# Another order of the ELU, the dot products and the weight rounding inside a dense step of a fused attention, MLP and expert kernel

## The chip, the cores and the metric

The kernel runs on one core of one Trainium2 chip. The time is device time in microseconds (us), from launch to end, of one execution; the figure for a kernel is the median of several executions. Five engines work side by side: TensorE (PE, with its weight loads shown as PEld), VectorE (DVE), ScalarE (ACT), GpSimd (POOL) and SyncE (SP), which issues most transfers. Each engine runs its own instructions in the order in which the program wrote them, and waits on semaphores for the others.

## The reference, cut to what matters

```python
def _attn_ref(q, k, v):      # 2 batches, 8 heads, 768 positions, 64 dims:
    ...                      # local window plus block summaries, softmax
def _moe_ref(x, w_in, w_out):            # 1536 tokens, 512 -> 2048 -> 512
    h = x @ w_in
    g = np.where(h > 0.0, h, alpha * (np.exp(np.minimum(h, 0.0)) - 1.0))
    return (g @ w_out).astype(np.float32)

def _moe2_ref(x, expert_emb, tau, w1, w2):   # 8 experts, 512 -> 1024 -> 512
    xn = x / (np.linalg.norm(x, axis=-1, keepdims=True) + 1e-06)
    en = expert_emb / (np.linalg.norm(expert_emb, axis=-1, keepdims=True) + 1e-06)
    logits = xn @ en.T / tau
    expert_idx = np.argmax(logits, axis=1)
    ...
    for e in range(E):
        h = np.maximum(x[mask] @ w1[e], 0.0)
        out[mask] = gate_w[mask, None] * (h @ w2[e])
```

The change lies in `_moe_ref` (the dense MLP with its ELU) and in the products with the expert embeddings that choose an expert for each token.

## The kernel before

Attention comes first, then 64 **dense steps**, then 64 **expert steps**. A dense step `g` takes one of four chunks of 384 tokens (batch 0 and 1, two chunks each) and one of 16 slices of 128 hidden units. Steps 32 to 47 are the first chunk of batch 1, steps 48 to 63 the second. Expert steps begin at `GD` = 64.

To keep 32-bit precision, every operand is split in a rounded part and the rest: `split_hi` (L186, ACT) writes the rounded weights, `split_lo` (L190, DVE or POOL) the difference. A product is then three matmuls: high by high, high by low, low by high. In a step

- `up` (L557 to L559) is the first product, 12 matmuls into a PSUM bank `hp`;
- the ELU of the step before (`prev`) follows: `act_a` (L564, ACT: the negative part of `hp` into a tile `e`), `act_b` (L569, ACT: the exponential), `act_max` (L573, DVE: the maximum with `hp`), `act_hi` (L577, ACT: the rounded activations `gt`), `act_lo` (L581, POOL: the rest of `gt`);
- `split_u` rounds the weights of the first product two steps ahead; call its parts u_hi (ACT) and u_lo (DVE);
- `split_d` rounds the weights of the second product, d_hi (ACT) and d_lo (POOL in most steps from 33 on, DVE in steps 55 to 57);
- `down` (L596 to L598) is the second product of step `g - 2`, 9 matmuls.

So the activations of step `s` are made while step `s + 1` is issued, and multiplied in step `s + 2`.

Beside this, `extra` holds work that is hung on a step: from step 33 on the dot products `y_dot` of finished outputs with the expert embeddings. An output tile is loaded from memory two steps earlier (`y_load`, SP, tile `yl`). At its first dot product ACT copies it to PSUM (`yp`, L636); each of eight dot products (L640, DVE) reads `yp` and the embeddings `en_b`; after the first, ACT squares it (`ysq`, L630). Steps 33 to 40 hold four dot products each, steps 41 to 46 three (the last of them one), steps 52 to 54 one, 55 to 59 four. Routing, scatter, gather and the transposes of the first expert slot are in `extra` too (steps 49 to 64).

The order inside a step is that of the code, for each engine: `up`, `act_a`, `split_u`, `split_d` of the step before, `act_b`, `act_c` (which is `act_max`, `act_hi`, `act_lo`), loads, `extra`, `down`. Every instruction waits in its engine's queue for those written ahead of it.

Of the kernel before, what the change touches and what calls it, by code (L numbers as in the profile page):

```python
# [81 lines left out]
def fused_kernel(ctx, tc, q, k, v, w_in, w_out, emb, tau, w1, w2, consts, toks, minit, out):  # L82
    nc = tc.nc
# [48 lines left out]
    VP, RAW, BITS = {}, {}, {}  # L132
# [25 lines left out]
    def conv_bits(f, *ops):  # L158

        for n, o in ops:  # L160
            if f not in VP:
                VP[f] = v_p.tile([P, PW], F32, tag="v", name="vt")
            raw = RAW[f, n]
            hi, lo = raw[:, :, 1], raw[:, :, 0]
            t = VP[f][:, n * 512:(n + 1) * 512].bitcast(I32)
            if o == 0:
                BITS[f, n] = bank("cv").bitcast(I32)
            m = BITS[f, n]
            if o == 0:
                nc.vector.tensor_scalar(out=m, in0=hi, scalar1=3, scalar2=None, op0=ALU.logical_shift_left)  # L170
            if o == 1:
                nc.vector.scalar_tensor_tensor(
                    out=m, in0=hi, scalar=-0x80000000, in1=m, op0=ALU.bitwise_and, op1=ALU.bitwise_or
                )
            if o == 2:
                nc.vector.scalar_tensor_tensor(  # L176
                    out=t, in0=lo, scalar=29, in1=m, op0=ALU.logical_shift_right, op1=ALU.bitwise_or
                )
# [4 lines left out]
    def split_hi(src, down=False):  # L183
        pool, tag = (late["p"], "wd") if down and late else (w_p, "w")
        wt = pool.tile([P, 2, 512], F32R, tag=tag, name="wt", bufs=5)
        nc.scalar.activation(out=wt[:, 0, :], in_=src, func=AF.Copy)  # L186
        return wt

    def split_lo(src, wt, eng):
        eng.tensor_tensor(out=wt[:, 1, :], in0=src, in1=wt[:, 0, :].bitcast(F32), op=ALU.subtract)  # L190

    def split(src, eng, down=False):
        wt = split_hi(src, down)
        split_lo(src, wt, eng)
        return wt
# [342 lines left out]
    class Dense:  # L538
# [5 lines left out]
            self.eng = nc.gpsimd if (b, c) == (0, 0) else nc.vector  # L544

        def split_u(self):
            self.u = split(VP[self.f][:, 0:512], self.eng)

        def split_d(self, pool):
            self.d = split(VP[self.f][:, 512:1024], nc.gpsimd if pool else self.eng, True)  # L550

        def up(self):
            wt, xt = self.u, XT[self.b, self.c]
# [306 lines left out]
    class Expert:  # L860
# [16 lines left out]
            self.v = t  # L877

        def split_u(self):
            self.u = split(self.v[:, 0:512], nc.vector)  # L880

        def split_d(self, pool=False):
            self.d = split(self.v[:, 512:1024], nc.gpsimd if pool else nc.vector, True)

        def up(self):
            wt, x = self.u, self.s.x
# [103 lines left out]
    steps = [Dense(b, c, f) for b in range(B) for c in range(NCH) for f in range(KF)]  # L990
# [86 lines left out]
    with tc.manual_schedule():  # L1077
# [10 lines left out]
        GD = len(steps)  # L1088
        steps += [None] * (B * NSTAT * KE)
        GN = len(steps)  # L1090
        extra = {}
# [70 lines left out]
        for i in range(1, B * NSTAT):  # L1162
            g = GD + i * KE
            slot_steps(i, max(g - LEAD - 2, g1 + 3 if i >= NSTAT else 0), max(g - 7, g1 + 8 if i == NSTAT else 0), g - 3)
        pool_d = [32 < g <= 48 or 48 < g < g0 + 6 or g0 + 9 <= g < GD or GD < g < g1 + 5 and (g - GD) % KE not in (2,) for g in range(GN + 2)]

        def load_piece(g):
            s, f = divmod(g - GD, KE)
            steps[g] = (Expert if slots[s].tiles == NT2 else Half)(slots[s], f)
            steps[g].load()  # L1170

        n_split = G0 + 1
        for g in range(G0, GN + 2):
            prev = steps[g - 1] if 0 <= g - 1 < GN else None
            if g < GN:
                steps[g].up()
            if prev:
                prev.act_a()
                if g > GD and not isinstance(prev, Half):
                    prev.act_c()  # L1180
            if g - 3 >= GD and steps[g - 3].f == KE - 1:
                steps[g - 3].s.put()
            while n_split <= min(g + (1 if g < KF else 2), GN - 1):
                steps[n_split].split_u()
                n_split += 1
            one = isinstance(prev, Half)
            if g == GN:
                prev.split_d()
            if one:
                prev.act_c()  # L1190
            if prev and g < GN:
                prev.split_d(pool_d[g] and not one)
            if g < KF - 2:
                conv_bits(g + 2, *ALL[:3])
            if prev:
                prev.act_b()
                if g <= GD:
                    prev.act_c()
            if GD <= g + LEAD < GN:
                load_piece(g + LEAD)  # L1200
            for fn in extra.get((g, False), []):
                fn()
            if g >= 2:
                steps[g - 2].down()
            for fn in extra.get((g, True), []):
                fn()
# [94 lines left out]
```

## Time and profile before

| what | value |
|---|---|
| median of 3 runs | 562.68 us (561.32 to 563.0) |
| profiled execution, its own time | 561.42 us |
| its span, first to last instruction | 559.6 us |
| PE busy (matmuls) | 517.4 us, 92% of the span |
| DVE busy | 425.7 us, 76% |
| ACT busy | 354.0 us, 63% |
| POOL busy | 270.7 us, 48% |
| mean granted TensorE clock | 0.984 |

Step 33 begins at 233.86 us of the span with its first L557 matmul, step 37 at 250.59, step 44 at 286.76, step 59 at 349.78; step 64, the first expert step, begins at 372.49. Matmuls overlap, so their busy time says little about pauses; the start of one step to the start of the next says how long a step held PE. In an answer on a stretch, a row's "idle" with an arrow names what ended the wait just before that instruction.

### The profile page before, as it was taken

The page shows a single profiled execution, that of the slowest core. Times are in us where ns is not written, and L with a number is a line of the kernel's source. Part 1 is how long each engine was busy: PE and PEld are TensorE (multiplying, and loading weights), DVE is VectorE, ACT ScalarE, POOL GpSimd, SP SyncE. Part 2 cuts the span into 40 slices and gives each one's busy share as a digit, 9 for nine tenths or more (in the row PEclk, how much of TensorE's full clock was granted, in tenths as well). Part 3 has the DMA queues.
Part 4 walks back from the last instruction along what each step waited for, and adds up shares of the span by engine and source line. Part 5 has one row for each costly group of instructions (what it writes and reads, how often), then busy time and mean ns, then how long its engine had stood idle before and what let it go on. Part 6 is the DMA issues. An engine that isn't in the chain of part 4 may idle for free.

```text
span 559.6 us, 10282 instructions
## 1 busy us (share of the span) xinstructions
PE 517.4 (92%) x3270; PEld 455.2 (81%) x3270; DVE 425.7 (76%) x1053; ACT 354.0 (63%) x870; POOL 270.7 (48%) x274
## 2 busy tenths in 40 slices
PE   4986898999899999998999999999999999999991
PEld 4765786879788898896888998889779989999980
DVE  4999999988997665488776488866899777656671
ACT  3888685666767675565476655665565586566570
POOL 1477686876385332344457546765376532121010
PEclk9999998999999999999999999999999999999997
DMA  8999865669302014020100223718946399965000
GB/s 216 205 262 218 301 216 201 177 168 218 108 1 53 20 35 169 20 77 19 37 2 2 75 57 95 249 54 281 340 163 208 111 339 316 335 215 181 20 29 14
DMA packets 98939, 81.28 MB, mean 145 GB/s; under 512 B 38159, under 2 KB 83599, under 8 KB 98368
## 3 DMA queue, kind: packets, MB, share of 16 engines
q1 hardware_dynamic: 96256, 73.72, 44.7%
q0 software_dynamic: 2624, 6.84, 3.4%
q8 instruction: 28, 0.46, 0.4%
q14 instruction: 31, 0.25, 0.2%
HBM read 73.03 MB, written 6.94 MB: 143 GB/s over the span
## 4 chain that ended last, share of the span: by engine, by line
PE 31%; issue 8%; DVE 7%; ACT 5%; POOL 3%; POOLq 0%; ACTq 0%; DVEq 0%
PE shp L891 3%; PE o L914 3%; PE shp L892 3%; PE shp L890 3%; PE o L915 3%; PE o L913 3%; DVE ydj L640 3%; POOL wt L190 2%; DVE e L573 2%; PE y L598 1%; ACT wt L186 1%; DVE wt L190 1%; PE y L596 1%; PE y L597 1%; ACT gt L577 1%
## 5 line engine op out<-in xcount | busy, mean ns | idle before, releaser
L581 POOL TENSOR_TENSOR gt<-e,gt 128x384 fp32r<-128x384 f32 x63 | 64.0, 1016 | 87.7 <-ACT gt L577 50.1
L190 POOL TENSOR_TENSOR wt<-vt,wt 128x512 fp32r<-128x512 f32 x60 | 79.5, 1333 | 39.4 <-ACT wt L186 35.1
L190 DVE TENSOR_TENSOR wt<-mv,wt 128x512 fp32r<-128x512 f32 x113 | 80.6, 750 | 15.3 <-ACT wt L186 8.2
L557 PE MATMUL hp<-xT,wt 128*128 128x384 f32 x256 | 86.8, 339 | 3.8 <-DVE vt L176 2.7
L186 ACT ACTIVATE wt<-vt 128x512 fp32r<-128x512 f32 x128 | 75.5, 626 | 21.9 <-PE y L598 11.9
L559 PE MATMUL hp<-xT,wt 128*128 128x384 f32 x256 | 86.8, 339 | 0.2
L558 PE MATMUL hp<-xT,wt 128*128 128x384 f32 x256 | 86.3, 337 | 0.6 <-DVE xT L456 0.6
L598 PE MATMUL y<-wt,gt 128*128 128x512 f32 x192 | 77.9, 406 | 3.0 <-POOL gt L581 2.0
L596 PE MATMUL y<-wt,gt 128*128 128x512 f32 x192 | 78.7, 410 | 1.8 <-ACT gt L577 1.8
L190 DVE TENSOR_TENSOR wt<-vt,wt 128x512 fp32r<-128x512 f32 x68 | 57.7, 861 | 29.4 <-ACT wt L186 29.2
L577 ACT ACTIVATE gt<-e 128x384 fp32r<-128x384 f32 x64 | 33.5, 524 | 71.2 <-DVE e L573 67.3
L597 PE MATMUL y<-wt,gt 128*128 128x512 f32 x192 | 76.3, 398 | 0.0
L186 ACT ACTIVATE wt<-mv 128x512 fp32r<-128x512 f32 x128 | 73.8, 629 | 0.0
L640 DVE SCALAR_TENSOR_TENSOR ydj<-yp,en_b 128x512 bf16<-128x512 f32 x72 | 46.4, 686 | 12.6 <-ACT yp L636 5.9
L890 PE MATMUL shp<-sx,wt 128*128 128x256 f32 x192 | 54.4, 283 | 1.0 <-DVE ydj L640 0.7
L891 PE MATMUL shp<-sx,wt 128*128 128x256 f32 x192 | 54.2, 282 | 0.3 <-DVE sx L845 0.3
L557 PEld LDWEIGHTS hp<-xT,wt 128*128 128x128 f32 x256 | 48.4, 189 | 7.4 <-issue 2.4
L892 PE MATMUL shp<-sx,wt 128*128 128x256 f32 x192 | 54.0, 281 | 0.0
L558 PEld LDWEIGHTS hp<-xT,wt 128*128 128x128 f32 x256 | 48.5, 189 | 3.5 <-DVE xT L456 0.9
L598 PEld LDWEIGHTS y<-wt,gt 128*128 128x128 f32 x192 | 36.5, 190 | 16.1 <-POOL gt L581 6.9
L559 PEld LDWEIGHTS hp<-xT,wt 128*128 128x128 f32 x256 | 48.3, 189 | 1.0 <-POOL wt L190 1.0
L400 ACT ACTIVATE pt<-pt,mn 128x120 f32<-128x120 f32 x96 | 36.6, 384 | 13.9 <-DVE mn L395 13.2
(175 smaller groups left out, 1194.6 us busy)
## 6 DMA issues: line engine op xcount, KB each, us to landing
mv<-in_moe_w_dram SPq DMA_DIRECT2D x128, 256.0 KB
rw<-in_moe_w_in_dram SPq DMA_DIRECT2D x16, 512.0 KB
rv<-in_moe_w_out_dram SPq DMA_DIRECT2D x13, 512.0 KB
vw<-in_v_dram SPq DMA_DIRECT2D x16, 240.0 KB
kn<-in_k_dram SPq DMA_DIRECT2D x16, 192.0 KB
qn<-in_q_dram SPq DMA_DIRECT2D x16, 192.0 KB
vst<-in_v_dram SPq DMA_DIRECT2D x4, 768.0 KB
y_d<-ysb SPq DMA_DIRECT2D x12, 256.0 KB
```

The costliest lines, as they stand in the source:

```text
L186: nc.scalar.activation(out=wt[:, 0, :], in_=src, func=AF.Copy)
L190: eng.tensor_tensor(out=wt[:, 1, :], in0=src, in1=wt[:, 0, :].bitcast(F32), op=ALU.subtract)
L557: nc.tensor.matmul(hp, wh, xt[:, 0, kk, :], start=(kk == 0), stop=False)
L558: nc.tensor.matmul(hp, wh, xt[:, 1, kk, :], start=False, stop=False)
L559: nc.tensor.matmul(hp, wl, xt[:, 0, kk, :], start=False, stop=(kk == KD - 1))
L581: eng.tensor_tensor(out=gt[:, 1, :], in0=self.e, in1=gt[:, 0, :].bitcast(F32), op=ALU.subtract)
L596: nc.tensor.matmul(yp, gh, woh, start=(f == 0), stop=False)
L597: nc.tensor.matmul(yp, gh, wol, start=False, stop=False)
L598: nc.tensor.matmul(yp, gl, woh, start=False, stop=(f == KF - 1))
L890: nc.tensor.matmul(hp, wh, x[:, 0, kk, :], start=(kk == 0), stop=False)
L891: nc.tensor.matmul(hp, wh, x[:, 1, kk, :], start=False, stop=False)
L892: nc.tensor.matmul(hp, wl, x[:, 0, kk, :], start=False, stop=(kk == KD - 1))
```

## The change

In steps 33 to 64 the order within a step is written anew. `act_b` comes right behind `act_a`; then the first half of the step's `extra`; then `act_max`; then u_hi, d_hi, `act_hi`, `act_lo`, d_lo, the loads, u_lo, and the second half of `extra`. The `split_d` of a step is now issued in the step itself and not in the next one: step 33 issues those of 32 and 33, and step 65 none. `split_u` and `split_d` are taken apart into a `_hi` and a `_lo` part for this, in the dense and the expert class alike. No instruction is added or left out.

```diff
+        ELU0 = 33
         for g in range(G0, GN + 2):
             prev = steps[g - 1] if 0 <= g - 1 < GN else None
+            dense = ELU0 <= g <= GD
+            one = isinstance(prev, Half)
+            todo = extra.get((g, False), [])
...
+            if dense:
+
+                prev.act_b()
+                for fn in todo[:len(todo) // 2]:
+                    fn()
+                prev.act_max()
+                todo = todo[len(todo) // 2:]
...
+            new = []
             while n_split <= min(g + (1 if g < KF else 2), GN - 1):
-                steps[n_split].split_u()
+                if dense:
+                    steps[n_split].split_u_hi()
+                    new.append(steps[n_split])
+                else:
+                    steps[n_split].split_u()
                 n_split += 1
...
-            if prev and g < GN:
+            if dense:
+                ds = steps[g if g > ELU0 else g - 1:g + 1]
+                for x in ds:
+                    x.split_d_hi()
+                prev.act_hi()
+                prev.act_lo()
+                for x in ds:
+                    x.split_d_lo(pool_d[g])
+            elif prev and g < GN and g != GD + 1:
                 prev.split_d(pool_d[g] and not one)
...
-            if prev:
+            if g < ELU0:
                 prev.act_b()
-                if g <= GD:
-                    prev.act_c()
+                prev.act_c()
             if GD <= g + LEAD < GN:
                 load_piece(g + LEAD)
-            for fn in extra.get((g, False), []):
+            for x in new:
+                x.split_u_lo()
+            for fn in todo:
                 fn()
```

On VectorE, step 37 (and the head of step 38) stands like this before. `wt` is the result of a weight rounding, here u_lo; `e` with `hp` is the maximum of step 36, `ydj` a dot product with the copy `yp`.

```order
L190 TENSOR_TENSOR wt_3052<-vt_1089,wt_3052 128x512
L573 SCALAR_TENSOR_TENSOR e_3050<-e_3050,hp_2994 128x384
L640 SCALAR_TENSOR_TENSOR ydj_3065,lr_2788<-yp_3063,en_b_2828 128x512
L640 SCALAR_TENSOR_TENSOR ydj_3069,lr_2788<-yp_3063,en_b_2828 128x512
L640 SCALAR_TENSOR_TENSOR ydj_3071,lr_2788<-yp_3063,en_b_2828 128x512
L640 SCALAR_TENSOR_TENSOR ydj_3073,lr_2788<-yp_3063,en_b_2828 128x512
L190 TENSOR_TENSOR wt_3103<-vt_1123,wt_3103 128x512
```

The same step of the changed kernel on VectorE, with the head of step 38:

```order
L654 SCALAR_TENSOR_TENSOR ydj_3058,lr_2788<-yp_3056,en_b_2828 128x512
L654 SCALAR_TENSOR_TENSOR ydj_3062,lr_2788<-yp_3056,en_b_2828 128x512
L587 SCALAR_TENSOR_TENSOR e_3053<-e_3053,hp_2997 128x384
L190 TENSOR_TENSOR wt_3065<-vt_1089,wt_3065 128x512
L654 SCALAR_TENSOR_TENSOR ydj_3074,lr_2788<-yp_3056,en_b_2828 128x512
L654 SCALAR_TENSOR_TENSOR ydj_3076,lr_2788<-yp_3056,en_b_2828 128x512
L654 SCALAR_TENSOR_TENSOR ydj_3107,lr_2788<-yp_3056,en_b_2828 128x512
```

Two dot products moved ahead of the maximum, and u_lo from ahead of the maximum to right behind it.

On ScalarE, step 37 before (`wt` here are u_hi and d_hi, in that order):

```order
L564 ACTIVATE e_3050<-hp_2994 128x384
L186 ACTIVATE wt_3052<-vt_1089 128x512
L186 ACTIVATE wt_3055<-vt_926 128x512
L569 ACTIVATE e_3050<-e_3050 128x384
L577 ACTIVATE gt_3060<-e_3050 128x384
L636 ACTIVATE yp_3063<-yl_2983 128x512
L630 ACTIVATE ysq_3067,ss_2787<-yp_3063 128x512
```

And in the changed kernel:

```order
L578 ACTIVATE e_3053<-hp_2997 128x384
L583 ACTIVATE e_3053<-e_3053 128x384
L650 ACTIVATE yp_3056<-yl_2986 128x512
L644 ACTIVATE ysq_3060,ss_2787<-yp_3056 128x512
L186 ACTIVATE wt_3065<-vt_1089 128x512
L186 ACTIVATE wt_3067<-vt_972 128x512
L591 ACTIVATE gt_3069<-e_3053 128x384
```

The exponential moved past both roundings, and the copy and the square past `gt`, which is now the step's last instruction on this engine; d_hi reads the next slice (`vt_972` for `vt_926`).

On GpSimd, steps 37 and 38 and the head of 39 before:

```order
L190 TENSOR_TENSOR wt_3055<-vt_926,wt_3055 128x512
L581 TENSOR_TENSOR gt_3060<-e_3050,gt_3060 128x384
L190 TENSOR_TENSOR wt_3106<-vt_972,wt_3106 128x512
L581 TENSOR_TENSOR gt_3111<-e_3101,gt_3111 128x384
L190 TENSOR_TENSOR wt_3149<-vt_1048,wt_3149 128x512
```

And in the changed kernel, from the last instruction of step 36 on:

```order
L190 TENSOR_TENSOR wt_3020<-vt_926,wt_3020 128x512
L595 TENSOR_TENSOR gt_3069<-e_3053,gt_3069 128x384
L190 TENSOR_TENSOR wt_3067<-vt_972,wt_3067 128x512
L595 TENSOR_TENSOR gt_3116<-e_3104,gt_3116 128x384
L190 TENSOR_TENSOR wt_3114<-vt_1048,wt_3114 128x512
```

Within a step d_lo stood ahead of the rest of `gt`; it now stands behind it, and belongs to the next slice.

## Rows read from the trace of the kernel before

**Rows 1.** Windows, four stretches of steps: us, busy us (and count) of each engine.

```profile
core 0: us, PE busy (x) PEld busy (x) DVE busy (x) ACT busy (x) POOL busy (x), PEclk, DMA share, GB/s
233.86:250.59 16.73, 16.73 (x86) 15.14 (x84) 11.95 (x31) 11.50 (x26) 7.52 (x7) 1.00 0.18 64
250.59:286.76 36.17, 33.37 (x148) 27.05 (x147) 30.27 (x73) 20.39 (x45) 18.16 (x16) 0.95 0.07 22
286.76:349.78 63.02, 63.02 (x328) 56.84 (x327) 45.05 (x129) 40.97 (x89) 37.19 (x37) 1.00 0.17 51
349.78:372.49 22.71, 22.45 (x115) 19.36 (x113) 16.33 (x34) 14.30 (x32) 17.27 (x16) 1.00 0.58 187
390.00:430.00 40.00, 37.76 (x249) 32.95 (x248) 38.06 (x91) 21.07 (x48) 21.92 (x20) 1.00 0.78 254
```

**Rows 2.** Timeline of TensorE: start us, us, line, operation, wait before it.

```profile
233.86 0.33 PE L557 MATMUL hp<-xT,wt 128*128 128x384 f32 x1
...
238.04 0.33 PE L557 MATMUL hp<-xT,wt 128*128 128x384 f32 x1
...
263.69 0.50 PE L596 MATMUL y<-wt,gt 128*128 128x512 f32 x1 [1.25 <-ACT gt L577]
...
364.93 0.60 PE L841 MATMUL stp<-cst,xg 128*128 128x128 f32 x4
...
372.49 0.39 PE L890 MATMUL shp<-sx,wt 128*128 128x256 f32 x1 [0.22 <-ACT sx L844]
373.21 0.39 PE L891 MATMUL shp<-sx,wt 128*128 128x256 f32 x1 [0.34 <-DVE sx L845]
```

**Rows 3.** Timeline of VectorE, ScalarE and GpSimd, steps 37 to 39.

```profile
251.76 0.54 DVE L573 SCALAR_TENSOR_TENSOR e<-e,hp 128x384 f32<-128x384 f32 x1
...
254.35 1.30 POOL L190 TENSOR_TENSOR wt<-vt,wt 128x512 fp32r<-128x512 f32 x1 [0.35 <-ACT wt L186]
...
254.67 1.53 DVE L190 TENSOR_TENSOR wt<-vt,wt 128x512 fp32r<-128x512 f32 x1
256.12 0.54 DVE L573 SCALAR_TENSOR_TENSOR e<-e,hp 128x384 f32<-128x384 f32 x1
...
257.80 0.69 DVE L640 SCALAR_TENSOR_TENSOR ydj<-yp,en_b 128x512 bf16<-128x512 f32 x1 [1.14 <-ACT yp L636]
...
258.54 0.60 ACT L630 ACTIVATE ysq<-yp 128x512 f32<-128x512 f32 x1 [0.77 <-DVE ydj L640]
...
259.26 0.69 DVE L640 SCALAR_TENSOR_TENSOR ydj<-yp,en_b 128x512 bf16<-128x512 f32 x1 [0.75 <-ACT ysq L630]
...
259.87 0.69 DVE L640 SCALAR_TENSOR_TENSOR ydj<-yp,en_b 128x512 bf16<-128x512 f32 x1
...
261.10 1.46 DVE L190 TENSOR_TENSOR wt<-vt,wt 128x512 fp32r<-128x512 f32 x1
262.48 0.54 DVE L573 SCALAR_TENSOR_TENSOR e<-e,hp 128x384 f32<-128x384 f32 x1
```

**Rows 4.** Groups by line in steps 33 to 43: busy us, mean ns, idle before.

```profile
L190 DVE TENSOR_TENSOR wt<-vt,wt 128x512 fp32r<-128x512 f32 x11 | 12.6, 1148 | 0.8 <-ACT wt L186 0.8
...
L581 POOL TENSOR_TENSOR gt<-e,gt 128x384 fp32r<-128x384 f32 x10 | 10.2, 1015 | 12.6 <-ACT gt L577 10.6 <-issue 1.7 <-POOL wt L190 0.3
...
L569 ACT ACTIVATE e<-e 128x384 f32<-128x384 f32 x11 | 5.7, 520 | 0.0
L564 ACT ACTIVATE e<-hp 128x384 f32<-128x384 f32 x10 | 4.8, 480 | 0.0
```

**Rows 5.** Tile `wt`, 232 to 256 us: ns min/median/max of the roundings on VectorE.

```profile
L190 DVE TENSOR_TENSOR wt<-vt,wt x5: 691/1467/1535, 233.6 to 254.7; 128x512 fp32r<-128x512 f32 x5
```

**Rows 6.** Timeline: an output tile's load on SyncE and its copy, steps 35 to 37.

```profile
243.47 0.32 SPq L616 DMA_DIRECT2D yl<-y_d  x1
...
246.40 0.59 ACT L636 ACTIVATE yp<-yl 128x512 f32<-128x512 f32 x1
```

**Rows 7.** Timeline of VectorE in step 61: one u_lo.

```profile
359.58 3.27 DVE L190 TENSOR_TENSOR wt<-vt,wt 128x512 fp32r<-128x512 f32 x1 [0.94 <-ACT wt L186]
```

More of the change, by code (lines that the diff above doesn't have):

```diff
@@ L546, in split_u, with split_u_hi, split_u_lo, split_d_hi @@
         def split_u(self):
[L547 to L550 removed]
+            self.split_u_hi()
+            self.split_u_lo()
+        def split_u_hi(self):
+            self.u = split_hi(VP[self.f][:, 0:512])
+        def split_u_lo(self):
+            split_lo(VP[self.f][:, 0:512], self.u, self.eng)
+        def split_d(self, pool):
+            self.split_d_hi()
+            self.split_d_lo(pool)
+        def split_d_hi(self):
+            self.d = split_hi(VP[self.f][:, 512:1024], True)
+        def split_d_lo(self, pool):
+            split_lo(VP[self.f][:, 512:1024], self.d, nc.gpsimd if pool else self.eng)
         def up(self):
@@ L879, in split_u, with split_u_hi, split_u_lo, split_d_hi @@
         def split_u(self):
-            self.u = split(self.v[:, 0:512], nc.vector)
-        def split_d(self, pool=False):
-            self.d = split(self.v[:, 512:1024], nc.gpsimd if pool else nc.vector, True)
+            self.split_u_hi()
+            self.split_u_lo()
+        def split_u_hi(self):
+            self.u = split_hi(self.v[:, 0:512])
+        def split_u_lo(self):
+            split_lo(self.v[:, 0:512], self.u, nc.vector)
+        def split_d(self, pool=False):
+            self.split_d_hi()
+            self.split_d_lo(pool)
+        def split_d_hi(self):
+            self.d = split_hi(self.v[:, 512:1024], True)
+        def split_d_lo(self, pool):
+            split_lo(self.v[:, 512:1024], self.d, nc.gpsimd if pool else nc.vector)
         def up(self):
@@ L1178, in fused_kernel @@
                 prev.act_a()
-                if g > GD and not isinstance(prev, Half):
+                if g > GD and not one:
                     prev.act_c()
+            if dense:
[4 more added lines that the diff above has]
+                todo = todo[len(todo) // 2:]
             if g - 3 >= GD and steps[g - 3].f == KE - 1:
                 steps[g - 3].s.put()
+            new = []
             while n_split <= min(g + (1 if g < KF else 2), GN - 1):
-                steps[n_split].split_u()
+                if dense:
[3 more added lines that the diff above has]
+                    steps[n_split].split_u()
                 n_split += 1
-            one = isinstance(prev, Half)
             if g == GN:
```

## Prediction

> **What bounds the kernel now.** I first looked at the windows of the steps that the change touches [rows 1] and at the starts of single steps on TensorE [rows 2]. Step 33 begins at 233.86 us and step 34 at 238.04: a step with nothing in its way takes 4.18 us. The windows give the rest by subtraction. Steps 33 to 36 take 16.73 us, which is 4 x 4.18: no pause. Steps 37 to 43 take 36.17, where 7 x 4.18 is 29.26: PE stands for **6.91 us**. Steps 44 to 58 take 63.02 against 62.70: nothing (the routing's few matmuls lie there). Steps 59 to 63 take 22.71 against 20.90, 1.81 more; two sets of four transposes lie in it, each busy for 0.60 us [rows 2], so 0.6 to 1.8 is pause, and I take **1.1**. At the first matmuls of step 64 PE waits 0.22 + 0.34 us [rows 2], **0.56**. In sum PE stands for about **8.6 us** between 233 and 374 us, and this is all that the change can win where it acts. Elsewhere in the stretch PE issues without a gap, so work taken from another engine there is worth nothing.
>
> Who makes PE wait? At 263.69 it waits 1.25 us for `gt` from ACT [rows 2], and `gt` is late because the maximum on DVE is. The timeline of DVE shows the beat: the maximum comes at 251.76, 256.12 and 262.48 [rows 3], so two steps with four dot products each take DVE 10.72 us, where PE needs 8.36. DVE falls behind by 1.18 us a step from step 33 on; once the lead of the first steps is used up (by step 37), PE waits. This lasts until the dot products become three a step (step 41). In the window of these stalls the granted TensorE clock averages 0.95, in the other stretches it is 1.00 [rows 1]: part of the 6.91 us is matmuls at the lower of the clock's two levels, 1.2 GHz, after the pause at 262 to 263 us, and goes with the pause.
>
> **What fills the 10.72 us** [rows 3]. Eight dot products, one every 0.61 us (259.26 to 259.87): 4.88. Two maxima at 0.54: 1.08. Two u_lo, 1.53 and 1.46: 2.99. One wait of 1.14 for the copy `yp` and one of 0.75 for the square, both on ACT. That is 10.84, and ends that overlap take 0.1 off.
>
> **The change, part by part.**
>
> *u_lo behind the maximum.* Now u_lo begins while POOL works on d_lo (254.35 to 255.65 against 254.67 to 256.20, [rows 3]). In this part of the trace it took 0.69 us at best and 1.47 in the median [rows 5], and over steps 33 to 43 1.148 in the mean, 11 times [rows 4]. In the new order POOL's block of a step starts with the rest of `gt`, which needs `gt` (0.53 us on ACT), which needs the maximum; u_lo starts directly at the maximum's end. So it has a lead of 0.5 us and needs 0.69, and POOL's block (1.02 + 1.30, [rows 3, 4]) is over 2.9 us behind the maximum, well ahead of the next. Bounds: 0.69 (alone) and 1.53 (as now). I take 0.69, since nearly all of it lies where POOL is idle: 2.99 becomes 1.38.
>
> The Trainium skill (SBUF — State Buffer, section "SBUF: two separate sides") says that VectorE and GpSimd share one pair of SBUF ports as an exclusive lock, taken for a whole instruction by a VectorE operation with two SBUF inputs. The trace agrees in kind, 0.69 against 1.47 us in rows 5; by the rule and by the rows the sum is the same as long as u_lo comes first, and the rule's other case is the third rival below.
>
> *The exponential first, the copy ahead of `gt`.* Now `yp` stands on ACT behind `gt`, and DVE idles 1.14 us from the maximum to the first dot product. In the new order DVE has u_lo and two dot products to do after the maximum (0.69 + 1.22 = 1.91 us), while ACT does `gt` (0.53), the negative part (0.48), the exponential (0.52, [rows 4]) and the copy (0.59, [rows 6]): 2.12. The wait falls from 1.14 to about 0.2; its bounds are 0 and 1.14.
>
> *The square* keeps its place between the first and second dot product: 0.75 as now.
>
> *Half the dot products ahead of the maximum.* They cost DVE nothing more, but the maximum, `gt`, its rest and `down` stand behind them, and behind `yp` and the square. What hides this: activations made in step s + 1 are needed in step s + 2, and PE has 2 x 4.18 = 8.36 us of other matmuls between. The chain in a step with a copy is 0.48 + 0.52 + 0.59 + 0.69 + 0.60 + 0.69 + 0.54 + 0.53 + 1.02 = 5.66 us, with about 0.1 for each of nine handovers (ysq begins 0.05 after the dot product's end, the next dot product 0.12 after ysq's, [rows 3]) 6.6. So 1.8 us to spare; without it each step would stop PE.
>
> *d_hi and d_lo one step earlier, d_lo behind the rest of `gt`.* Their number stays, and d_lo's 1.30 us [rows 3]; the weights are ready a step sooner, and `gt`'s rest no longer stands behind 1.30 us of d_lo. Step 33 rounds two slices (about 0.6 us more on ACT, an estimate from the copy of as many elements, [rows 6]), and step 65 none; ACT is busy 11.5 of 16.7 us there [rows 1] and hides it. Zero either way.
>
> *Loads.* `y_load` keeps its place, two steps ahead; SP is passed by nothing else that PE waits for. Scatter and gather on POOL (steps 55 to 59) now stand ahead of the rest of `gt`; POOL is busy 37 of 63 us there [rows 1], and the spare time covers them.
>
> **Sum.** Two steps on DVE: 4.88 + 1.08 + 1.38 + 0.2 + 0.75 = 8.29 us against PE's 8.36. DVE stops falling behind, though by a hair. Of the 6.91 us I count 6.6; 0.3 is left for step 40, which has the small normalising operations on DVE besides its four dot products. Of 1.1 + 0.56 in steps 59 to 64 I count 1.2: there too u_lo meets POOL (one took 3.27 us, [rows 7]) and the maximum and the slot's copies stand behind the roundings. Together **7.8 us**. The profiled execution took 561.42 us, 1.26 less than the median of the three runs (562.68) and inside their spread: 553.6 by its own time, 554.9 by the median. I say **554.3 us**.
>
> **Rivals.**
> 1. *The forecast.* DVE keeps PE's beat. 554.3 us; chance 0.66.
> 2. *u_lo still meets POOL as now.* If u_lo keeps about 1.5 us (POOL's block of the step before not over, or u_hi late), two steps take 8.29 + 1.6 = 9.9 us, 1.5 too long; four such pairs (steps 33 to 40) make 6.2, less the 1.8 to spare 4.4 us of PE waits, 4.1 more than forecast: 558.4 us. For it: the beat fits by only 0.07 us. Against: POOL's block ends 1.3 us before the next maximum. Chance 0.18.
> 3. *Slower: u_lo falls behind POOL's joined block.* Where u_lo starts more than about 0.5 us behind the maximum, the rest of `gt` and d_lo are on POOL one behind the other, and u_lo ends only after both, 2.3 us later; the 3.27 us of rows 7 is such a case. In steps 33 to 40 a pair would take 8.29 + 4.6 = 12.9 us, 4.5 too long, 18 for the four pairs less 1.8: 16 us of waits where 6.6 were to be won, about 570 us. It decides if u_hi, which stands ahead of `gt` on ACT, is not done when the maximum ends. Against it: u_hi, about as long as the copy (0.59 us, [rows 6]), follows the exponential or the square at once. Chance 0.04. It is the lock of the Trainium skill's page on SBUF taken by the other side first.
> 4. *A late tile in front of the maximum (slower).* Each of nine `yl` loads now stands ahead of a maximum. To end 0.3% above before, they would have to come some 1.1 us beyond the spare 1.8 each: 564.4 us. Against it: one issued at 243.47 was used at 246.40 [rows 6], 2.9 us at most, and two steps are 8.4. Chance 0.03.
> 5. *Won and given back.* From 390 to 430 us DVE is busy 38.06 of 40 us [rows 1]; if expert steps that start 8 us sooner only wait longer there, 561 to 562 us. Against it: that work hangs on steps and moves along with them. Chance 0.07.
>
> The remaining 0.02 I spread.
>
> **How the numbers follow.** About 0.3% (1.7 us) is what a measurement of this kernel can tell from no change. Faster are 1 and 2 and a little of the rest: 0.86; no change is 5: 0.07; slower 3 and 4: 0.07. The range begins where all 8.6 us go and some of the small waits behind step 64 with them, 552.2, and ends at the second rival with the copy's wait at its upper bound, 558.8; it leaves out 3, 4 and 5.
>
> **What would show each step.** In the profile after: steps 37 to 43 in some 29.5 us and the clock at 1.00 throughout; u_lo at 0.7 us in the mean instead of 1.148; maxima two steps apart by 8.4 us; the first dot product's wait for `yp` near 0.2; `gt` on ACT waiting little for the maximum. If PE still waits for `gt` in steps 38 to 42, step 2 holds; if it waits for weights (`wt` from DVE), step 3. The prediction is wrong if the expert steps take longer than before from start to end, or if dot products wait for a load.

## The result, and the profile after

The changed kernel takes **553.0 us** in the median of 4 runs (552.34 to 555.01), the kernel before 562.62 us (561.32 to 563.0, 4 runs beside it): a ratio of 0.9839, 95% interval 0.9807 to 0.9871, **1.6% faster**. Run a second time with other kernels it gave 554.16 us, ratio 0.9848 (0.9814 to 0.9883). Its profiled execution took 553.61 us with a span of 551.8; before, 561.42 and 559.6. So the span is 7.8 us shorter.

The windows of the changed kernel, the same five stretches as [rows 1] (steps 33 to 36, 37 to 43, 44 to 58, 59 to 63, and 40 us of expert steps):

```profile
core 0: us, PE busy (x) PEld busy (x) DVE busy (x) ACT busy (x) POOL busy (x), PEclk, DMA share, GB/s
234.12:250.85 16.73, 16.73 (x86) 15.14 (x85) 14.82 (x39) 13.82 (x31) 9.06 (x8) 1.00 0.18 64
250.85:280.06 29.21, 29.21 (x149) 26.41 (x147) 25.65 (x70) 20.91 (x46) 17.94 (x17) 1.00 0.09 28
280.06:343.08 63.02, 63.02 (x329) 56.85 (x327) 49.58 (x126) 42.33 (x87) 37.99 (x38) 1.00 0.20 59
343.08:364.85 21.77, 21.77 (x114) 19.62 (x113) 13.57 (x30) 14.14 (x30) 13.56 (x13) 1.00 0.51 172
382.40:422.40 40.00, 37.71 (x248) 32.91 (x247) 38.06 (x92) 21.19 (x48) 21.87 (x20) 1.00 0.77 254
```

Steps 37 to 43 take 29.21 us, which is 7 x 4.18 within 0.05, where they took 36.17: PE no longer stands, and the granted clock is 1.00 where it was 0.95. That is 6.96 us. Some 1.7 of them are the clock, an estimate from this window of the kernel before (columns as above): right behind PE's waits in step 39 TensorE ran 3.42 us at a granted 0.50, the lower of the clock's two levels (1.2 GHz), in place of 1.00.

```profile
264.84:268.26 3.42, 3.42 (x9) 2.74 (x10) 2.58 (x6) 1.37 (x4) 1.42 (x2) 0.50 0.24 77
```

Steps 59 to 63 take 21.77 for 22.71, 0.94 less, and PE is busy all of it, so what is above 20.90 is the transposes. The other stretches are as long as before. Step 64 waits once instead of twice [rows 2] (timeline of TensorE):

```profile
364.85 0.28 PE L918 MATMUL shp<-sx,wt 128*128 128x256 f32 x1
...
365.47 0.39 PE L919 MATMUL shp<-sx,wt 128*128 128x256 f32 x1 [0.34 <-DVE sx L859]
```

From the first matmul of step 33 to that of step 65 it is 134.85 us, where it was 142.87: **8.0 us** gained, some 6.3 of pauses and 1.7 of clock. Step 33 itself began 0.26 us later (234.12 for 233.86). From step 65 to the end of the span nothing changed (182.83 us and 182.87).

The beat of VectorE, and GpSimd beside it, against [rows 3] (timeline, two steps with four dot products each):

```profile
253.34 0.55 DVE L587 SCALAR_TENSOR_TENSOR e<-e,hp 128x384 f32<-128x384 f32 x1
...
253.81 0.68 DVE L190 TENSOR_TENSOR wt<-vt,wt 128x512 fp32r<-128x512 f32 x1
...
254.41 0.68 DVE L654 SCALAR_TENSOR_TENSOR ydj<-yp,en_b 128x512 bf16<-128x512 f32 x1
...
254.53 1.02 POOL L595 TENSOR_TENSOR gt<-e,gt 128x384 fp32r<-128x384 f32 x1 [2.36 <-ACT gt L591]
...
255.51 1.29 POOL L190 TENSOR_TENSOR wt<-vt,wt 128x512 fp32r<-128x512 f32 x1
...
256.86 0.55 DVE L587 SCALAR_TENSOR_TENSOR e<-e,hp 128x384 f32<-128x384 f32 x1
...
257.32 0.68 DVE L190 TENSOR_TENSOR wt<-vt,wt 128x512 fp32r<-128x512 f32 x1
...
259.42 0.69 DVE L654 SCALAR_TENSOR_TENSOR ydj<-yp,en_b 128x512 bf16<-128x512 f32 x1 [0.20 <-ACT yp L650]
...
260.87 0.69 DVE L654 SCALAR_TENSOR_TENSOR ydj<-yp,en_b 128x512 bf16<-128x512 f32 x1 [0.75 <-ACT ysq L644]
...
261.49 0.55 DVE L587 SCALAR_TENSOR_TENSOR e<-e,hp 128x384 f32<-128x384 f32 x1
```

From maximum to maximum two steps later it is 8.15 us (253.34 to 261.49; 8.21 one step earlier), where it was 10.72 and PE needs 8.36. Each u_lo takes 0.68, directly behind the maximum; the first ends at 254.49, GpSimd starts at 254.53 and is done at 256.80, ahead of the next u_lo at 257.32. The wait for `yp` is 0.20, that for the square 0.75 as before.

The groups by line in steps 33 to 43 (against [rows 4]):

```profile
L595 POOL TENSOR_TENSOR gt<-e,gt 128x384 fp32r<-128x384 f32 x11 | 11.5, 1047 | 19.3 <-ACT gt L591 11.8 <-issue 6.1 <-PE hp L573 0.9
L190 DVE TENSOR_TENSOR wt<-vt,wt 128x512 fp32r<-128x512 f32 x11 | 8.6, 784 | 0.0
...
L591 ACT ACTIVATE gt<-e 128x384 fp32r<-128x384 f32 x11 | 5.7, 522 | 6.0 <-DVE e L587 6.0
```

The mean u_lo is 784 ns, 1148 before. Two are long: in step 34 (1.21 us), where GpSimd still works on the second d_lo of step 33, and in step 42 (1.26 us), whose maximum comes only 2.3 us behind that of step 41, so that GpSimd still works on step 41's d_lo.

### The profile page after: what moved, and what is told of

It is laid out like the page before. It is cut to its first block, busy times and chain, and to the rows that moved or that the text cites. A ratio compares the mean times of both kernels' runs of the same rounds, so it can differ in the third digit from the quotient of the medians.

```text
span 551.8 us, 10263 instructions
## 1 busy us (share of the span) xinstructions
PE 511.1 (93%) x3270; PEld 453.2 (82%) x3270; DVE 425.7 (77%) x1053; ACT 357.1 (65%) x870; POOL 268.5 (49%) x274
## 4 chain that ended last, share of the span: by engine, by line
PE 66%; DVE 14%; issue 6%; DMA 4%; ACT 3%; SPq 3%; POOL 3%; POOLq 0%; ACTq 0%; DVEq 0%
PE y L610 6%; PE y L612 6%; PE y L611 6%; PE hp L573 6%; PE hp L571 6%; PE hp L572 6%; PE shp L919 4%; PE shp L920 4%; PE shp L918 4%; PE o L942 3%; PE o L943 3%; PE o L941 3%; DVE cv L172 3%; DVE cv L170 3%; PE sc L383 2%
## 5 line engine op out<-in xcount | busy, mean ns | idle before, releaser
L595 POOL TENSOR_TENSOR gt<-e,gt 128x384 fp32r<-128x384 f32 x63 | 65.3, 1036 | 108.0 <-ACT gt L591 62.1
L190 DVE TENSOR_TENSOR wt<-mv,wt 128x512 fp32r<-128x512 f32 x114 | 81.9, 755 | 14.1 <-ACT wt L186 12.2
L610 PE MATMUL y<-wt,gt 128*128 128x512 f32 x192 | 77.6, 404 | 1.7 <-ACT gt L591 1.7
L612 PE MATMUL y<-wt,gt 128*128 128x512 f32 x192 | 76.1, 397 | 1.6 <-DVE gt L595 0.8
L611 PE MATMUL y<-wt,gt 128*128 128x512 f32 x192 | 75.6, 394 | 0.0
L190 DVE TENSOR_TENSOR wt<-vt,wt 128x512 fp32r<-128x512 f32 x67 | 51.7, 785 | 14.3 <-ACT wt L186 14.1
```

The costliest lines, as they stand in the source:

```text
L595: eng.tensor_tensor(out=gt[:, 1, :], in0=self.e, in1=gt[:, 0, :].bitcast(F32), op=ALU.subtract)
L610: nc.tensor.matmul(yp, gh, woh, start=(f == 0), stop=False)
L611: nc.tensor.matmul(yp, gh, wol, start=False, stop=False)
L612: nc.tensor.matmul(yp, gl, woh, start=False, stop=(f == KF - 1))
```

## The experiments

All are told as changes of the changed kernel, and timed against the kernel before in the same set. "Pair" is the time from a maximum to the one two steps later, around 248 to 262 us; "33 to 64" is from the first matmul of step 33 to that of step 65, in the profiled execution. In this stretch the granted clock is 1.00 in all of them but two, the kernel before and e3: 142.87 and 140.02 hold some 1.7 us of the lower clock each.

| kernel | time, us | ratio to before (95%) | pair, us | 33 to 64, us |
|---|---|---|---|---|
| before | 562.2 to 562.6 in the sets | 1 | 10.72 | 142.87 |
| changed | 553.0 | 0.9839 (0.9807 to 0.9871) | 8.15 to 8.21 | 134.85 |
| changed, again (e9) | 554.16 | 0.9848 (0.9814 to 0.9883) | as above | 134.86 |
| e1 d early alone | 561.78 | 0.9986 (0.9968 to 1.0005) | 9.56 | 141.89 |
| e2 d as before | 557.44 | 0.9906 (0.9874 to 0.9939) | 8.30 | 138.17 |
| e3 u_lo behind dots | 558.82 | 0.9930 (0.9906 to 0.9953) | 8.73 | 140.02 |
| e4 maximum first | 555.33 | 0.9871 (0.9841 to 0.9901) | 8.50 | 135.91 |
| e5 all dots first | 562.12 | 0.9993 (0.9976 to 1.0010) | 9.43 | 143.02 |
| e7 d late, behind `gt` | 554.87 | 0.9870 (0.9839 to 0.9901) | 8.14 to 8.20 | 135.53 |
| e8 d early, ahead of `gt` | 557.69 | 0.9913 (0.9884 to 0.9942) | 8.30 | 138.24 |
| e10 u_lo and d alone | 560.06 | 0.9947 (0.9926 to 0.9968) | 8.51 | 140.10 |
| e11 u_lo ahead | 564.23 | 1.0041 (1.0025 to 1.0058) | 9.34 | 145.70 |
| e12 exponential and dots alone | 558.18 | 0.9927 (0.9907 to 0.9946) | 8.89 | 138.86 |
| e6 two dots per expert step | 556.74 | 0.9894 (0.9877 to 0.9911) | 8.15 to 8.21 | 134.84 |

### First set: one part at a time

Theory A is the prediction's: VectorE's beat decides. Rival B: the order on GpSimd (rest of `gt` ahead of d_lo). Rival C: the dot products ahead of the maximum.

**e1**, only the second product's roundings moved; exponential, maximum, u_lo and dot products stand as before:

```diff
-                prev.act_b()
-                for fn in todo[:len(todo) // 2]:
-                    fn()
-                prev.act_max()
-                todo = todo[len(todo) // 2:]
...
-                    steps[n_split].split_u_hi()
-                    new.append(steps[n_split])
+                steps[n_split].split_u()
...
-                prev.act_hi()
-                prev.act_lo()
+                prev.act_b()
+                prev.act_c()
```

> Only the second product's weights move (rounded for the step itself, their rest behind the rest of gt on GpSimd); the exponential, the maximum, u_lo and the dot products stand as before. Theory A (VectorE's beat of two four-dot steps against TensorE's 8.36 us): u_lo now comes 2.5 us and more behind the maximum, when GpSimd's block is over or nearly so, and falls to about 0.7 to 1.1 us; the wait for yp stays at 1.14. Beat 9.2 to 9.7 us, 3.5 to 5.3 us too long over four pairs, less some 3.5 us to spare in the old, shorter chain: 0 to 2 us of TensorE waits in steps 37 to 43, time 553.5 to 556 us. Theory B (GpSimd's order: the rest of gt stood behind d_lo): everything is won, 553 us.

No faster. The pair fell to 9.56 us, since u_lo now meets GpSimd only in every other step, and the expected beat was right; but both theories missed the time. Spare time did not hide the 1.2 us by which the beat is still too long: PE waits in steps 39 and 41 for both halves of `gt`, and in steps 43, 45, 58, 60 and 61 for the rest of it (timeline of TensorE, step 39):

```profile
263.48 0.50 PE L610 MATMUL y<-wt,gt 128*128 128x512 f32 x1 [0.30 <-ACT gt L591]
...
264.58 0.50 PE L612 MATMUL y<-wt,gt 128*128 128x512 f32 x1 [0.36 <-POOL gt L595]
```

B falls: by steps 33 to 64 this order on GpSimd alone is worth 1.0 us of 8.0, and that is less than the 1.7 us that the kernel before lost to the clock.

**e2**, all but the roundings of the second product:

```diff
-                ds = steps[g if g > ELU0 else g - 1:g + 1]
-                for x in ds:
-                    x.split_d_hi()
+                prev.split_d(pool_d[g])
                 prev.act_hi()
                 prev.act_lo()
-                for x in ds:
-                    x.split_d_lo(pool_d[g])
-            elif prev and g < GN and g != GD + 1:
+            elif prev and g < GN:
```

> The reverse: exponential first, half the dot products ahead of the maximum, u_lo behind it, but the second product's weights still rounded in the step after, their rest ahead of the rest of gt on GpSimd. Theory A: u_lo still starts at the end of the maximum with GpSimd idle or only just starting, beat 8.3 to 9 us, no waits of TensorE in steps 37 to 43: 553 to 555 us. Theory B: d_lo's 1.3 us stand ahead of the rest of gt as before, so the gain of this stretch (7 us) is lost: about 560 us.

557.44 us, between the two. The pair is 8.30, as the beat asks, and yet 3.3 us of the 8.0 are lost, in steps 36 (0.5), 42 (1.8, two steps behind the normalising operations) and 63 (0.9). The prediction had put this edit at nothing. In one step of two d_lo starts with u_lo as the maximum ends, and takes 1.84 us; in the other d_lo is already at work (from 250.94) and u_lo waits (timeline):

```profile
251.66 1.12 DVE L190 TENSOR_TENSOR wt<-vt,wt 128x512 fp32r<-128x512 f32 x1
...
256.45 0.69 DVE L190 TENSOR_TENSOR wt<-vt,wt 128x512 fp32r<-128x512 f32 x1
...
256.45 1.84 POOL L190 TENSOR_TENSOR wt<-vt,wt 128x512 fp32r<-128x512 f32 x1 [2.79 <-ACT wt L186]
...
258.25 1.02 POOL L595 TENSOR_TENSOR gt<-e,gt 128x384 fp32r<-128x384 f32 x1
...
276.90 0.50 PE L611 MATMUL y<-wt,gt 128*128 128x512 f32 x1 [0.68 <-POOL wt L190]
...
277.88 0.50 PE L612 MATMUL y<-wt,gt 128*128 128x512 f32 x1 [0.47 <-POOL gt L595]
```

Two explanations were left: the weights are a step late (L), or d_lo stands in the wrong place (O). e7 and e8 tell them apart.

**e3**, u_lo behind the second half of the dot products, where GpSimd is at work:

```diff
-            for x in new:
-                x.split_u_lo()
             for fn in todo:
                 fn()
+            for x in new:
+                x.split_u_lo()
```

> As the changed kernel, but u_lo stands behind the second half of the step's extra work, some 1.2 us behind the maximum, where GpSimd runs the rest of gt and d_lo one behind the other. Theory A with the port held by whole instructions: u_lo takes 1.7 to 2.4 us in the four-dot steps, the beat is 10.3 to 11.6 us, 2 to 3.2 too long, 8 to 13 over four pairs, less 1.8 to spare: 6 to 11 us of TensorE waits, 559 to 564 us. Theory B, or a port that costs VectorE little when it comes second: 553 us.

558.82 us, just below the 559 to 564 of theory A, but not by its way: u_lo took 1.12 us and not 1.7 to 2.4, and the pair is 8.73 and not 10.3 to 11.6 (timeline of VectorE and GpSimd):

```profile
255.10 1.02 POOL L595 TENSOR_TENSOR gt<-e,gt 128x384 fp32r<-128x384 f32 x1 [2.05 <-issue]
...
255.55 1.12 DVE L190 TENSOR_TENSOR wt<-vt,wt 128x512 fp32r<-128x512 f32 x1
...
256.08 1.74 POOL L190 TENSOR_TENSOR wt<-vt,wt 128x512 fp32r<-128x512 f32 x1
```

It waits for the rest of `gt` (to 256.12) and ends 0.55 us later; d_lo then takes 1.74 instead of 1.30. VectorE gets in between two instructions of GpSimd and loses 0.43 us a step, not the 2.3 of the prediction's third rival. The lock that the Trainium skill describes (SBUF — State Buffer, section "SBUF: two separate sides"), held for one instruction, fits these rows. Of the 5.2 us that e3 loses to the changed kernel, 3.8 lie in steps 42 and 43, behind waits of 0.94 and 0.73 us for `gt`, and by estimate 1.7 of these are the clock (a window as above), so the time came near by luck:

```profile
277.42:280.83 3.41, 3.41 (x11) 3.03 (x10) 3.41 (x7) 2.52 (x6) 2.99 (x3) 0.50 0.04 7
```

**e4**, no dot product ahead of the maximum:

```diff
-                for fn in todo[:len(todo) // 2]:
-                    fn()
                 prev.act_max()
-                todo = todo[len(todo) // 2:]
```

> As the changed kernel, but all of the step's extra work stands behind the maximum. Theory A: the copy yp is behind gt on ScalarE again, the wait of about 1 us comes back, beat about 9.0 us, 0.6 too long, 2.6 us over four pairs; the chain to gt is 2 us shorter, with some 4 us to spare, so TensorE waits for nothing: 553 us. Theory C (the gain comes from the dot products ahead of the maximum, with the copy early): the waits of steps 37 to 43 come back in part, 556 us or more.

555.33 us, between A and C: the pair is 8.50, since the wait for `yp` is 0.48 instead of 0.20 and its square's 0.82 for 0.75. Halving the dot products is worth some 1.1 us in steps 33 to 64 (135.91 against 134.85).

### Second set: where the dot products and d_lo stand

e9 is the changed kernel unaltered.

> The changed kernel once more, unaltered, so that the three others of this set have it beside them on the same chip. All theories: 553 us, steps 33 to 64 in 134.9 us, no pause of PE in steps 37 to 43.

554.16 us; steps 33 to 64 took 134.86 us, and no step from 33 to 43 more than 4.18.

**e5**, all dot products ahead of the maximum:

```diff
-                for fn in todo[:len(todo) // 2]:
+                for fn in todo:
                     fn()
                 prev.act_max()
-                todo = todo[len(todo) // 2:]
+                todo = []
```

> The changed kernel with all dot products of a step (not half of them) ahead of the maximum. VectorE's work is the same, the maximum and all that hangs on it come about 1.2 us later in every step with four dot products. By the prediction's chain (6.6 us of 8.36, 1.8 us to spare) this costs nothing or little: 553 to 555 us, the pair of maxima still 8.2 to 8.5 us apart. If the chain was really at its end (the spare time was too large in the run that moved only the second product's weights), each of steps 34 to 43 loses up to a microsecond: 558 us or more, with waits for gt from ACT and POOL.

All is lost again, 562.12 us. The expectation overlooked a wait: with nothing but u_lo behind the maximum, VectorE has no work while ScalarE makes `gt`, the negative part, the exponential and `yp`:

```profile
264.06 0.69 DVE L654 SCALAR_TENSOR_TENSOR ydj<-yp,en_b 128x512 bf16<-128x512 f32 x1 [1.42 <-ACT yp L650]
```

The pair is 9.43, and PE waits in steps 34, 38 and 40 to 42, and in 56, 57, 59 and 60. So the run does not test the spare time by itself; it shows that the half behind the maximum is what covers the chain on ScalarE.

**e7 and e8** complete a table with e2: when the second product's weights are rounded, and whether d_lo stands behind the rest of `gt`. e7 (late, behind) and e8 (early, ahead):

```diff
 e7
-                ds = steps[g if g > ELU0 else g - 1:g + 1]
-                for x in ds:
-                    x.split_d_hi()
+                prev.split_d_hi()
                 prev.act_hi()
                 prev.act_lo()
-                for x in ds:
-                    x.split_d_lo(pool_d[g])
-            elif prev and g < GN and g != GD + 1:
+                prev.split_d_lo(pool_d[g])
+            elif prev and g < GN:
 e8
                 for x in ds:
-                    x.split_d_hi()
+                    x.split_d(pool_d[g])
                 prev.act_hi()
                 prev.act_lo()
-                for x in ds:
-                    x.split_d_lo(pool_d[g])
```

> The changed kernel, but a step rounds the second product's weights of the step before, as the kernel before did, with d_lo behind the rest of gt as in the changed kernel. Theory L (what made the run with the old rounding slow, 557.4 us, is that the weights are ready a step later, too late for the second product): 557 us or more, since d_lo now ends even later, with PE waits for wt from POOL. Theory O (it is the place of d_lo ahead of the rest of gt, beside u_lo): 553 to 554 us, u_lo 0.69 us and d_lo 1.3 us in every step.

> The changed kernel with the weights of the second product a step early as there, but d_lo on GpSimd ahead of the rest of gt as in the kernel before. Theory L: 553 to 554 us, since no weight is late. Theory O: 557 us, d_lo and u_lo start together at the end of the maximum, u_lo takes 1.1 us or d_lo 1.8 in turns, and the rest of gt comes late: PE waits for gt from POOL in steps 37 to 43.

O holds: e7 gave 554.87 us and e8 557.69. By steps 33 to 64, d_lo behind the rest of `gt` is worth 138.24 - 134.85 = 3.4 us with early weights and 138.17 - 135.53 = 2.6 with late ones; a step earlier is worth 0.7 behind and nothing ahead. PE's wait in step 42 (timelines of TensorE), first in e7, then in e8:

```profile
274.30 0.50 PE L611 MATMUL y<-wt,gt 128*128 128x512 f32 x1 [0.37 <-POOL wt L190]
```

```profile
277.53 0.50 PE L612 MATMUL y<-wt,gt 128*128 128x512 f32 x1 [1.42 <-POOL gt L595]
```

### Third set: the two terms alone, and the next bound

**e10** keeps u_lo behind the maximum and the new place of the second product's roundings, but the exponential stands behind the two roundings, and the copy and all dot products behind `gt`, as before:

```diff
             if dense:
-                prev.act_b()
-                for fn in todo[:len(todo) // 2]:
-                    fn()
-                prev.act_max()
-                todo = todo[len(todo) // 2:]
...
-                prev.act_hi()
-                prev.act_lo()
+                prev.act_b()
+                prev.act_c()
```

> The kernel before with two parts of the change alone: u_lo behind the maximum, and the second product's weights a step earlier with d_lo behind the rest of gt. The exponential, the copy yp and all dot products stay where they were (behind gt). It prices the first term of the sum by itself (2.99 to 1.38 us for each two steps). Theory A (the beat of VectorE decides): u_lo 0.69 us; the wait for yp shrinks by the u_lo that now lies in it, 1.14 to about 0.5; two steps take 4.88 + 1.08 + 1.38 + 0.5 + 0.75 = 8.6 us against 8.36, four such pairs fall 1 us behind, inside the spare time: 553 to 555 us. Theory C (the copy and the halves of the dot products are needed as well): 556 us or more.

The beat came as worked out: 8.51 to 8.56 us for 8.6, with u_lo at 0.68. The time did not: 560.06 us. Up to step 41 every step takes 4.18 us, but steps 42 and 43 together 2.2 us more, and steps 57 to 61 together 3.2 us more; theory C's figure, 556 us or more, holds. In step 58 the maximum itself waits, for the exponential that stands behind two roundings on ScalarE, and the rest of `gt` is late (timelines of VectorE and of TensorE):

```profile
345.01 0.56 DVE L587 SCALAR_TENSOR_TENSOR e<-e,hp 128x384 f32<-128x384 f32 x1 [0.52 <-ACT e L583]
```

```profile
347.69 0.50 PE L612 MATMUL y<-wt,gt 128*128 128x512 f32 x1 [0.77 <-POOL gt L595]
```

e4 has the same beat (8.50) and differs from e10 by this alone: there the exponential and the maximum stand ahead of u_hi and d_hi. It took 4.2 us less in steps 33 to 64 (135.91 against 140.10). The lead is made in step 34, whose maximum waits for the exponential (timelines of VectorE, first in e10, then in e4):

```profile
243.40 0.55 DVE L587 SCALAR_TENSOR_TENSOR e<-e,hp 128x384 f32<-128x384 f32 x1 [1.30 <-ACT e L583]
```

```profile
240.54 0.56 DVE L587 SCALAR_TENSOR_TENSOR e<-e,hp 128x384 f32<-128x384 f32 x1 [0.41 <-ACT e L583]
```

That is 7.69 us behind the first matmul of step 33 (235.71) in e10 and 6.07 (234.47) in e4. With the same beat e10's maxima stay 1.6 us late in their steps, up to the waits of step 42.

**e11** puts u_lo ahead of the maximum again, all else as changed; **e12** takes e11 and rounds the second product's weights as before (as in e2), so that of the change only the exponential, the copy and the halved dot products are left.

```diff
             if dense:
                 prev.act_b()
                 ...
-                prev.act_max()
+            while n_split <= min(g + (1 if g < KF else 2), GN - 1):
+                steps[n_split].split_u()
+                n_split += 1
+            if dense:
+                prev.act_max()
...
-            for x in new:
-                x.split_u_lo()
```

> The changed kernel with u_lo ahead of the maximum again. Theory P (u_lo became short because it stands directly behind the maximum): 1.1 us and more in the mean, two steps 9.5 us, 557 us or more. Theory O (it became short because d_lo went behind the rest of gt, so that GpSimd is idle around the maximum on either side): 0.69 to 0.75 us; but the wait for yp grows by the 0.6 us that u_lo no longer covers, 0.2 to 0.8, so two steps take 8.9 us: 553.5 to 555.5 us.

> The kernel before with the exponential, the copy and half the dot products ahead of the maximum alone: u_lo stands ahead of the maximum and d_lo of the step before ahead of the rest of gt, as they did. It prices the second term of the sum by itself (the wait for yp, 1.14 to 0.2). Theory A: u_lo starts beside d_lo as before, 1.5 us where they meet; two steps take 4.88 + 1.08 + 2.99 + 0.2 to 0.8 + 0.75 = 9.9 to 10.5 us, 558 to 561 us. Theory O: d_lo starts when its d_hi is done, behind u_hi, so that it meets u_lo in every step: the upper half of that, 559 to 562 us.

e11 is **slower than the kernel before**, 564.23 us, though its pair is 9.34 us and not 10.72. Every other u_lo falls on the end of d_lo, and the maximum stands behind it:

```profile
259.58 1.30 POOL L190 TENSOR_TENSOR wt<-vt,wt 128x512 fp32r<-128x512 f32 x1
...
260.28 1.15 DVE L190 TENSOR_TENSOR wt<-vt,wt 128x512 fp32r<-128x512 f32 x1
...
261.36 0.54 DVE L587 SCALAR_TENSOR_TENSOR e<-e,hp 128x384 f32<-128x384 f32 x1
...
264.04 0.69 DVE L654 SCALAR_TENSOR_TENSOR ydj<-yp,en_b 128x512 bf16<-128x512 f32 x1 [0.93 <-ACT yp L650]
```

PE waits for the rest of `gt` in steps 36, 38, 40, 41 and 42 (0.36 us each in the timeline, and each of these steps lasts 0.6 to 1.2 us longer than 4.18). What the beat lacks to 8.36 is felt at once; still, steps 37 to 43 take 33.12 us, 3.0 less than before. What makes e11 slower lies behind them: steps 44 to 58 take 66.63 us (63.02 before) and steps 59 to 63 24.22 (22.71), with waits for the rest of `gt` in steps 45, 54, 56, 58 and 60. Why it is late there was not taken apart; e12, with the same order on VectorE, takes 63.02 and 22.31. Theory P was nearer; the short u_lo of theory O held in one step of two.

e12 took 558.18 us, at the lower end of the expectation, because u_lo waited for nothing: u_hi and d_hi follow each other on ScalarE, so that d_lo can only start after u_lo has begun (around the pair u_lo takes 0.69 us each, d_lo 1.37 to 1.60; timeline of VectorE and GpSimd):

```profile
251.37 0.69 DVE L190 TENSOR_TENSOR wt<-vt,wt 128x512 fp32r<-128x512 f32 x1
...
251.62 1.60 POOL L190 TENSOR_TENSOR wt<-vt,wt 128x512 fp32r<-128x512 f32 x1 [0.90 <-ACT wt L186]
...
254.67 0.69 DVE L654 SCALAR_TENSOR_TENSOR ydj<-yp,en_b 128x512 bf16<-128x512 f32 x1 [0.93 <-ACT yp L650]
```

The pair is 8.89. By steps 33 to 64 e12 is worth 142.87 - 138.86 = 4.0 us and e10 2.8; some 1.7 in each is the lower clock that only the kernel before had. Neither prices one term of the sum. In e12 the wait for `yp` fell only from 1.14 to 0.93, and most of what its pair is shorter, 1.6 of 1.8 us, is u_lo again. In e10 u_lo now stands between the maximum and the first dot product and covers part of the wait for `yp`. The two terms were not priced apart.

**e6**: two dot products in each expert step from 66 on.

```diff
-        g1 = tails([(1, 1)], T2, lambda g: 3 - g % 2)
+        g1 = tails([(1, 1)], T2, lambda g: 2)
```

> The changed kernel with two dot products in each of the expert steps from 66 on, where it has three and two in turns, so that they last 16 steps and not 13. VectorE is busy 38.1 of 40 us there and PE waits for a dot product (0.73 us) and others, 2.7 us in all between 382 and 402 us. If VectorE's load makes these waits: 551 to 552 us. If they hang on the single late tile, or the routing that comes three steps later is waited for: 553 us or more.

The waits between 382 and 407 us are gone, as this one of the changed kernel (timelines of TensorE, here and of e6 below):

```profile
385.13 0.38 PE L918 MATMUL shp<-sx,wt 128*128 128x256 f32 x1 [0.73 <-DVE ydj L654]
```

But the routing comes later, and the gather behind it makes PE wait longer than all of them:

```profile
451.59 1.12 PE L855 MATMUL stp<-cst,xg 128*128 128x128 f32 x4 [4.62 <-DMA xg<-y_d,mt]
```

556.74 us, 0.9894 against the changed kernel's 0.9848 and 0.9839. None of the versions is faster than the changed kernel.

## Why the prediction was right, and what it had wrong

**The time and its sum held.** The forecast was 554.3 us; 553.0 and, the second time, 554.16 were measured. Counted were 6.6 + 1.2 = 7.8 us; the span is 7.8 us shorter and the profiled execution took 553.61 us where 553.6 stood in the sum. That they agree so closely is luck. By place: 6.96 in steps 37 to 43 (6.6 counted), 0.94 in steps 59 to 63 and some 0.1 in step 64 (1.2 counted together), 0.3 lost ahead of step 33. The 0.3 kept back for step 40 was not needed: the normalising operations cost VectorE more there than before (below), but the spare time took them. That part of the pause was the lower clock and would go with it held too, with some 1.7 us.

**u_lo behind the maximum, 2.99 to 1.38 for two steps.** Measured 1.36. The reason given, that GpSimd is idle there, is the right one, and e2, e3 and e8 show the price when it is not: 1.12 for 0.69. The place behind the maximum is not the only one: in e12 u_lo stands ahead of it and takes 0.69 as well, because it starts ahead of d_lo.

**The wait for `yp`, 1.14 to 0.2.** Measured 0.20 and 0.26. The way it was worked out, ScalarE's chain from the maximum to the copy less VectorE's work meanwhile, holds in the other orders too: 2.1 us of chain less two dot products gave 0.93 (e12), less u_lo alone 1.42 (e5), and where the copy follows `gt` directly, some 1.1 us less u_lo, 0.48 (e4, e10).

**"They cost DVE nothing more": half the dot products ahead of the maximum, 1.8 us to spare.** In the changed kernel the rest of `gt` of the late step ends at 255.55 and is first read in step 38, whose second product starts at 257.10 and reads it 0.46 us in: 2.0 us to spare. That was right, for this order. It is no reserve that many steps can draw on: e1 and e11, whose pairs are 1.2 and 1.0 us too long, lost 3.8 and 3.9 us to the changed kernel in steps 37 to 43 alone.

**The step that failed: "d_hi and d_lo one step earlier, d_lo behind the rest of `gt` ... Zero either way."** e2 and e8 show 2.6 to 3.4 us. Not the earlier step is worth them (0.7 or nothing), but d_lo's place. Where d_lo stands ahead and u_lo behind the maximum, they meet in every step, one of the two waits for the other, and in one step of two the rest of `gt` begins 2.3 us behind the maximum (255.99 to 258.25 in e2) instead of 1.2 (253.34 to 254.53). The prediction used this clearance in its term for u_lo, without seeing that it came from this edit; so the sum was right and the share was not. And the parts do not add: u_lo ahead or behind the maximum and d_lo ahead or behind the rest of `gt` give 558.18 (e12, both ahead), 564.23 (e11, only d_lo moved), 557.69 (e8, only u_lo moved) and 553.0 (both). In e12 the roundings also belong to the step before; with d_lo ahead that made no difference between e2 and e8.

**A step that was priced by half: "the exponential first".** The prediction gave it one effect, the shorter wait for `yp`. e4 and e10 have that wait alike (0.48) and the same beat, and are 4.2 us apart: with the exponential behind the roundings the maximum itself comes late, in step 34 by 1.6 us, and the beat does not make it up. The 4.2 us lie in steps 42 to 58; in steps 59 to 63 e10 is not slower (22.87 us against 23.02).

**The rivals.** The second (u_lo still meets GpSimd, 558.4 us) did not happen but for the two long u_lo of steps 34 and 42. e2 and e8, where the two meet in every step, came near its time (557.4 and 557.7) by another way: u_lo took 0.69 and 1.12 in turns, not 1.5, and the pair was 8.30, not 9.9; what came late was the rest of `gt`. The third (570 us) priced a collision at 2.3 us a step; e3 measured 0.43, and 558.8. The fourth did not show: no dot product or maximum waited for a load. The fifth did not either: expert steps took as long as before.

**What stays open.** e1's beat is 1.2 us shorter than before, and yet its pauses are not: the 1.0 us that it won in steps 33 to 64 is less than the 1.7 us of lower clock that it was spared. Its waits show where (steps 39 to 45 and 58 to 61), but how much of each is the late exponential (worth 4.2 us between e10 and e4) and how much the u_lo ahead of the maximum was not taken apart. Nor was what e11 lost from step 44 on. And the runs do not tell what brings the lower clock: it came behind waits of PE of 1.25 and 0.35 us in the kernel before and of 0.94 and 0.73 us in e3, and not behind the one of 1.42 us in e8.

## What to carry to other kernels

When a vector engine falls behind a little in each step, add up its busy time and its waits over one repeat of the steps and compare with the engine that should be the bound; then ask where in the step the operation stands on which that engine waits, because the same beat with a late release can lose much of the gain (e10 beside e4). Two instructions on VectorE and GpSimd that block each other are best placed together: counted from e12, moving the one on GpSimd alone lost 6.0 us, moving the one on VectorE alone won 0.5, and moving both won 5.2. Work hung between an operation and its answer from another engine is cover; all of it on one side leaves the other bare (e5).

## What the runs showed of the hardware that was not expected

- **A tiny operation waits too.** The first normalising operation, 128 x 3, took 0.16 us before and 1.20 us in the changed kernel, where it starts 0.13 us behind a d_lo and ends with it (264.98 and 264.95; timelines of VectorE before, then of GpSimd and VectorE in the changed kernel):

```profile
273.71 0.16 DVE L655 TENSOR_SCALAR ss<-ss 128x3 f32<-128x3 f32 x1
```

```profile
263.65 1.30 POOL L190 TENSOR_TENSOR wt<-vt,wt 128x512 fp32r<-128x512 f32 x1
...
263.78 1.20 DVE L669 TENSOR_SCALAR ss<-ss 128x3 f32<-128x3 f32 x1
```

- **In two places VectorE did not get in between.** In e3 u_lo ended 0.55 us after the GpSimd instruction that it met, although another followed. In the kernel before [rows 7] one took 3.27 us, and in e1 one 3.12: each ended 0.56 us after the last of three instructions of GpSimd, one behind the other. The timeline of e1:

```profile
359.80 1.01 POOL L841 DMA_INDIRECT xg<-y_d,mt  x1 [0.30 <-issue]
...
360.52 3.12 DVE L190 TENSOR_TENSOR wt<-vt,wt 128x512 fp32r<-128x512 f32 x1 [0.88 <-ACT e L578]
...
360.83 1.02 POOL L595 TENSOR_TENSOR gt<-e,gt 128x384 fp32r<-128x384 f32 x1
...
361.79 1.29 POOL L190 TENSOR_TENSOR wt<-vt,wt 128x512 fp32r<-128x512 f32 x1
```

  Both times GpSimd had issued an indirect transfer just before, in e1 still when u_lo began; whether that is the reason was not tried. The Trainium skill's rule that the lock is held for one instruction (same page and section) does not give these two times.
